# A recurrent attention layer and a soft-max feed-forward layer on one core: the same work in another written order

## The chip, the cores and the metric

The kernel runs on one core of one Trainium2 chip. Time is device microseconds (us) from the first to the last instruction of a run; the figure for a kernel is the median of its runs. A core has five engines with a queue each: TensorE (PE, matrix products into the banks of PSUM), VectorE (DVE), ScalarE (ACT), GpSimd (POOL) and SyncE (SP, which here only issues transfers). Each engine works through its queue in order and waits at an instruction until what it needs is there.

## The reference

Two layers, one after the other. The first is a linear recurrence over 768 steps for 4 batches and 8 heads of 48 columns; the second is a feed-forward layer over the 3072 tokens that come out.

```
for t in range(S):
    cur = einsum('bhd,bhe->bhde', u * k[t], v[t])
    y[t] = einsum('bhd,bhde->bhe', r[t], state + cur)
    state = w[t][..., None] * state + einsum('bhd,bhe->bhde', k[t], v[t])
x = y laid out as tokens x 384
h = x @ w_in                                   # 384 -> 1024
solu = h * softmax(h)
ln = (solu - mean(solu)) / sqrt(var(solu) + 1e-6) * g_ln
out = ln @ w_out                               # 1024 -> 384
```

Inputs and output are float32; the products are taken in bf16.

## The kernel before, in words

The recurrence is cut into chunks of 128 steps: 6 chunks for each of 4 batches make 24 units, numbered chunk by chunk, so that unit i needs the state that unit i-4 left. Every unit goes through some 35 stages, and every stage is a small function that issues its instructions on one engine. Nothing is looped over units in the code: the string ORDER at the top lists about 900 words, one for a stage of a unit, and the last loop of the kernel calls the stages in this order. `InOrder` ties every instruction of an engine to the one before it, so the words of one engine are its program, word for word. The order was found by a search outside the kernel, against a model of the engines' and the transfers' times.

A word is a stage name, a unit and, after a dot, a letter or a PSUM slot. The letters a, d, p, s name the engine or queue (ACT, DVE, POOL, SP). The slots s0 to s3 are single PSUM banks, b0 and b1 are pairs of banks. A slot is free for its next tile only when the last reader of the tile before it is done, so the slots too tie the engines together. The stages that matter:

- LW, LK, LR, LV: the loads of w, k, r and v of one unit (192 KB each; functions `load_w` to `load_v`, from line 230). LI and LO load the weights, LU and LG the small vectors.
- lw (ACT, logarithm), cum (PE, two products of 384 columns), ex (ACT, exponential inside the bank), kp (DVE, decay times k and r; `scaled`, line 313).
- p, q (POOL), dg (DVE), dv (POOL): the bonus term with u; vb (ACT or POOL): v cast to bf16.
- krk, krr (PE, four transposes each, line 335) and kr (ACT or DVE, the copy out of PSUM, line 350). For some units KD takes their place: a transposing transfer issued by SP (line 441).
- M (PE, eight products, line 354), m (DVE with the mask in it, or ACT followed by sel on POOL), Y (PE, `attend`, line 376), y (line 398). With the letter i in Y's word, dv enters as one more product of 384 columns and y is a plain copy on ACT; without it, y on DVE adds dv.
- S (PE), et (ACT), st (DVE): the state.
- X (PE) and xT (copy), or XD (a transposing transfer): y turned for the second layer.
- H (PE, `hidden`, line 458), e (ACT, exponential), he (DVE, h times e), hq (ACT, square). For the units that have a word HD (14 to 22) H is laid out by token, SP turns he by a transposing transfer (line 469), and the sums of e and of the squares come from ACT.
- Oa, Ob (PE, the two halves of the output product, line 495), sq (ACT), qm (DVE), lv (ACT), o (ACT or DVE) and out (the store). Unit 23, the last, is done in smaller pieces: Ha, Hb, ea, eb, hea, heb, hqa, hqb, Sa, Sb for the sums, and Mal, Mbl, Mar, Mbr for the left and right columns of its output.
- gw (ACT or POOL), mn (PE), ce (DVE), wi: the weights with the gain g_ln in them, less their column means, cast to bf16; once, in the first 40 us.
- hot: `warm_up` (line 292), dummy products of 512 columns on zeros, whose result nobody reads. They keep PE busy in the head, where its real work has gaps. hot3.s0 is three of them in bank s0.

Buffers go round: 7 for the loads, 10 for lw and vb, 6 for kp, kr and dv, 4 for the rest (line 71).

Of the kernel before, what the change touches and what calls it, by code (L numbers as in the profile page):

```python
# [31 lines left out]
e3 Oa0.s1 p6 y4.a LR9.s kr6.d cum7.b0 lw8 Oa1.s0 vb6.p he3 et4 ex7 dv5 Ob0 LW10.s hq2 q6 kp7 X4.s3 hq3 LK10.s
M5.b1 p7 xT4.d M6.b0 m5.d krk7.s3 Ob1 sq0 m6.a q7 LR10.s qm0 dg6 krr7 lw9 cum8.b1 LV8.p kr7.d lv0 H4.b0 LW11.s
ex8 st4 p8 dg7 sq1 o0.a LK11.s Y5.ns3 qm1 kp8 e4 Oa2.s2 out0.p LR11.s y5.d q8 krk8.s1 lv1 cum9.b1 he4 krr8 LV9.s
ex9 Ob2 p9 kr8.d lw10 S5.s3 p10 hq4 kp9 Oa3.s1 LW12.s sel6 sq2 o1.d et5 lw11 M7.b0 LK12.s M8.b1 qm2 st5 m7.a Ob3
dv6 m8.d lv2 q9 cum10.b0 LR12.s sq3 X5.s0 Y6.ns3 o2.d ex10 vb7.p cum11.b1 xT5.d S6.s2 vb8.a out1 sel7 qm3 kp10
ex11 Oa4.s0 y6.d LW13.s LV10.p et6 lv3 H5.b0 st6 lw12 dg8 LK13.s o3.a dv7 kp11 X6.s3 krk9.s1 e5 LV11.p LR13.s
krk10.s2 krr9 xT6.d cum12.b1 dg9 LW14.s kr9.a Ob4 q10 he5 ex12 Y7.is3 LK14.s LV12.p dg10 krk11.s1 sq4 y7.a krr10
kp12 krr11 p11 kr10.a M9.b0 LR14.s S7.s3 m9.d dv8 H6.b1 hq5 p12 qm4 kr11.d et7 LW15.s lv4 S8.s2 st7 e6 vb9.p
X7.s1 o4.d LK15.s M10.b0 dv9 Y8.ns3 et8 xT7.d lw13 krk12.s0 he6 m10.a Oa5.s1 out2.p LR15.s vb10.p krr12 lw14  # L40
y8.d cum13.b0 p13 H7.b1 st8 LW16.s ex13 kr12.d q11 hq6 kp13 LK16.s S9.s3 LV13.p Y9.ns2 e7 dg11 LV15.s M11.b0
y9.d LV14.p X8.s0 Ob5 et9 m11.a he7 vb11.p krk13.s2 LR16.s lw15 M12.b0 q12 st9 xT8.a cum14.b1 m12.d sq5 krr13
LW17.s ex14 X9.s0 vb12.p Oa6.s3 sel10 xT9.a qm5 kp14 LK17.s cum15.b0 lv5 Ob6 dv10 ex15 kr13.d S10.s0 lw16 p14
kp15 hq7 M13.b1 LR17.s Y10.ns2 q13 H8.b0 sq6 et10 vb13.a qm6 o5.d LW18.s sel11 lv6 y10.d m13.a krk14.s1 st10
LK18.s Oa7.s2 q14 dg12 e8 o6.d krr14 LR18.s dv11 Y11.ns0 kr14.d lw17 cum16.b1 dv12 X10.s3 he8 Ob7 ex16 LW19.s
p15 S11.s1 LV16.s sq7 y11.d xT10.a H9.b0 hq8 out3.p kp16 LV17.s p16 et11 st11 X11.s0 H10.b1 e9 LK19.s dg13 p17
xT11.d lw18 qm7 he9 LR19.s q15 Y12.ns3 vb14.a krk15.s1 e10 S12.s0 vb15.p out4 y12.d krr15 dv13 lv7 M14.b0 kr15.d
Oa8.s3 m14.a sel13 he10 out5 X12.s1 lw19 M15.b0 LW20.s q16 et12 Ob8 m15.a st12 LK20.s dg14 p18 cum17.b1 dg15
H11.b0 out6 ex17 xT12.d sel14 o7.d hq9 kp17 out7 krk16.s0 Y13.ns1 vb16.p LR20.s sq8 e11 krr16 dv14 qm8 H12.b1
LW21.s kr16.d q17 hq10 y13.d LK21.s he11 krk17.s2 dv15 Oa9.s0 e12 LR21.s vb17.p Y14.ns1 lv8 he12 krr17 LW22.s  # L50
o8.a M16.b0 Ob9 lw20 kr17.d m16.a out8 cum18.b1 y14.d X13.s3 Oa10.s2 ex18 dg16 xT13.d dv16 sq9 hq11 S13.s1 kp18
X14.s3 sel15 M17.b0 xT14.d et13 hq12 KD18 Ob10 qm9 m17.d p19 cum19.b1 S14.s3 st13 ex19 q18 H13.b0 lv9 kp19 sel16
sq10 o9.a Y15.ns1 et14 e13 out9 st14 H14.b1 p20 LV18.s y15.d lw21 qm10 LV19.s he13 Oa11.s0 LK22.s e14 dg17
X15.s3 cum20.b0 lv10 xT15.d Y16.ns1 he14 Ob11 o10.a ex20 out10 vb18.p S15.s2 y16.d dv17 KD19 sq11 S16.s3 kp20
et15 hq13 cum21.b1 q19 S17.s1 qm11 st15 LV20.s H15.b0 et16 lv11 q20 st16 LR22.s ex21 dg18 vb19.a krk20.s2 kp21
Oa12.s3 et17 e15 st17 KD21 M18.b1 o11.a krr20 he15 X16.s1 Ob12 m18.a LW23.s kr20.d S18.s0 xT16.a HD14 sel18 sq12
lw22 M19.b0 qm12 M20.b1 m19.d Y17.ns2 m20.a vb20.p LK23.s Oa13.s1 dv18 LR23.s lv12 dg19 cum22.b0 y17.d H16.b1
dv19 LV21.s ex22 o12.d sel20 et18 kp22 X17.s2 HD15 S19.s3 e16 st18 p21 Ob13 xT17.d et19 he16 krk22.s0 p22 sq13
lw23 M21.b0 krr22 m21.a Y18.ns2 st19 q21 HD16 cum23.b1 qm13 kr22.d Y19.ns3 ex23 sel21 H17.b0 y18.d LV22.s lv13
y19.d o13.a kp23 X18.s0 Oa14.s2 e17 xT18.d KD23 M22.b1 dg20 Ob14 hq14 he17 dv20 X19.s3 Y20.ns1 vb21.p hq15  # L60
Oa15.s0 dg21 HD17 q22 y20.d H18.b0 xT19.d sq14 hq16 dv21 m22.d XD20 Ob15 p23 e18 dg22 Y21.ns1 out11 qm14 H19.b1
# [564 lines left out]
```

## Time and profile before

| | |
|---|---|
| time, median of 3 runs | 146.9 us (146.39 to 147.08) |
| span of the profiled execution | 144.8 us |
| PE busy | 132.1 us, 91% |
| DVE busy | 126.3 us, 87% |
| ACT busy | 123.8 us, 85% |
| POOL busy | 102.2 us, 71% |
| moved by transfers | 30.65 MB, mean 212 GB/s |
| mean granted TensorE clock | 0.988 |

How to read it. "Busy" is the time in which an engine has at least one instruction in flight. The page cuts the span into 40 slices of 3.6 us and gives the busy share of each in tenths; the same in microseconds can be had for any stretch. A table of waits says for which instruction an engine stood idle and whose end released it. The chain is followed back from the last instruction, at each step to what released it or to the instruction before it on its engine: what stands on it set the end of the run. In the rows of the timeline the first number is the start in us from the span's start, the second the duration, and a bracket at the end gives the idle time of the engine before it. Nearly all instructions carry line 88, that of the helper `InOrder`, so the rows are told apart by their tiles: o_ps is the output product, h_ps the hidden product, kr_ps the transposes, cum_ps the decays, m_ps the scores, y_ps and s_ps the attention output and the state, warm_ps the dummy products.

### The profile page before, as it was taken

The page shows a single profiled execution, that of the slowest core. Times are in us where ns is not written, and L with a number is a line of the kernel's source. Part 1 is how long each engine was busy: PE and PEld are TensorE (multiplying, and loading weights), DVE is VectorE, ACT ScalarE, POOL GpSimd, SP SyncE. Part 2 cuts the span into 40 slices and gives each one's busy share as a digit, 9 for nine tenths or more (in the row PEclk, how much of TensorE's full clock was granted, in tenths as well). Part 3 has the DMA queues.
Part 4 walks back from the last instruction along what each step waited for, and adds up shares of the span by engine and source line. Part 5 has one row for each costly group of instructions (what it writes and reads, how often), then busy time and mean ns, then how long its engine had stood idle before and what let it go on. Part 6 is the DMA issues. An engine that isn't in the chain of part 4 may idle for free.

```text
span 144.8 us, 4709 instructions
## 1 busy us (share of the span) xinstructions
PE 132.1 (91%) x1824; PEld 95.7 (66%) x1832; DVE 126.3 (87%) x239; ACT 123.8 (85%) x269; POOL 102.2 (71%) x128
## 2 busy tenths in 40 slices
PE   6699848896999999999999999999999999999781
PEld 2135537675978778987789788777676656557460
DVE  7154999699999999999999999989999998998651
ACT  3457687798899999999998999988997999999881
POOL 5269989897892999999999997594459777300000
PEclk9999996999999999999999999999999999999999
DMA  4999999999999979999989979649699997976934
GB/s 93 269 260 263 304 400 363 235 206 217 260 187 231 240 161 239 237 210 217 238 166 233 256 193 201 153 100 203 144 219 161 217 132 174 229 174 121 250 142 163
DMA packets 105623, 30.65 MB, mean 212 GB/s; under 512 B 100553, under 2 KB 104402, under 8 KB 105602
## 3 DMA queue, kind: packets, MB, share of 16 engines
q1 hardware_dynamic: 100192, 26.12, 83.1%
q0 software_dynamic: 1088, 3.34, 7.3%
q10 hardware_dynamic: 4322, 0.89, 2.9%
q8 instruction: 14, 0.23, 0.7%
q14 instruction: 7, 0.06, 0.1%
HBM read 22.03 MB, written 4.72 MB: 185 GB/s over the span
## 4 chain that ended last, share of the span: by engine, by line
PE 80%; DVE 8%; DMA 6%; issue 2%; ACT 1%; SPq 0%; DVEq 0%
PE o_ps L88 24%; PE h_ps L88 21%; PE kr_ps L88 7%; PE cum_ps L88 6%; PE y_ps L88 6%; PE m_ps L88 6%; PE s_ps L88 6%; DMA hq<-he 3%; DMA w_in<-in_w_dram 3%; PE warm_ps L88 3%; PE x_ps L88 2%; DVE m L88 2%; DVE kp L88 2%; DVE w L88 1%; DVE he L88 1%
## 5 line engine op out<-in xcount | busy, mean ns | idle before, releaser
L88 DVE TENSOR_TENSOR he<-h_ps,e 128x1024 bf16<-128x1024 f32 (+1 forms) x25 | 29.4, 1177 | 1.8 <-ACT e L88 1.2
L88 PE MATMUL o_ps<-w,he 128*128 128x385 bf16 (+2 forms) x136 | 29.2, 306 | 0.4 <-DVE qm L88 0.4
L88 DVE TENSOR_TENSOR kp<-cum_ps,kr_in 128x768 bf16<-128x768 f32 x24 | 22.8, 952 | 5.2 <-ACT cum_ps L88 3.6
L88 ACT ACTIVATE e<-h_ps 128x1024 bf16<-128x1024 f32 (+1 forms) x25 | 24.7, 989 | 2.9 <-PE h_ps L88 2.7
L88 POOL TENSOR_TENSOR p<-kr_in 128x384 bf16<-128x384 f32 x24 | 23.9, 1003 | 4.3 <-DMA kr_in<-in_k_dram 2.9
L88 PEld LDWEIGHTS <-hq 128*128 128x128 bf16 x192 | 17.9, 97 | 12.6 <-DMA hq<-he 1.2
L88 POOL TENSOR_TENSOR dv<-vb,dg 128x384 bf16<-128x384 bf16 x24 | 19.9, 830 | 6.5 <-DVE dg L88 5.5
L88 PE MATMUL h_ps<-xT,win_sb 128*128 128x128 bf16 x360 | 23.4, 223 | 0.6 <-DVE kp L88 0.6
L88 ACT ACTIVATE cum_ps<-cum_ps 128x768 f32<-128x768 f32 x24 | 19.2, 799 | 4.3 <-PE cum_ps L88 3.6
L88 PEld LDWEIGHTS <-win_sb 128*128 128x128 bf16 x360 | 21.8, 100 | 1.5 <-issue 0.7
L88 POOL TENSOR_TENSOR q<-p,u_bc 128x384 bf16<-128x384 bf16 x24 | 21.8, 913 | 0.1
L88 PE MATMUL o_ps<-inv_col,e 128*128 128x1 bf16 x120 | 19.3, 165 | 0.0
L88 PE MATMUL o_ps<-one_col,hq 128*128 128x1 bf16 x120 | 19.1, 163 | 0.0
L88 PEld LDWEIGHTS <-kp 128*128 128x128 bf16 x240 | 15.5, 99 | 4.9 <-DVE xT L88 1.7
L88 DVE TENSOR_TENSOR m<-m_ps,uts 128x1024 bf16<-128x1024 f32 x13 | 15.8, 1219 | 2.4 <-PE m_ps L88 2.4
L88 PE MATMUL kr_ps<-ident,kp 128*128 128x128 bf16 x160 | 15.2, 226 | 1.6 <-DVE xT L88 1.6
L88 ACT ACTIVATE hq<-he 128x1024 bf16<-128x1024 bf16 (+1 forms) x16 | 15.9, 1003 | 0.0
L88 ACT ACTIVATE lw<-w_in 128x384 bf16<-128x384 f32 x24 | 12.6, 527 | 3.2 <-DMA w_in<-in_w_dram 3.2
L88 PE MATMUL o_ps<-w,hq 128*128 128x385 bf16 x72 | 13.9, 328 | 0.8 <-DMA hq<-he 0.8
L88 POOL TENSOR_SCALAR_AFFINE_SELECT m<-m 128x1024 bf16<-128x1024 bf16 x11 | 12.0, 1088 | 3.6 <-ACT m L88 3.6
L88 PEld LDWEIGHTS <-kr 64*128 64x128 bf16 (+1 forms) x272 | 10.7, 96 | 4.8 <-issue 1.1
L88 DVE TENSOR_REDUCE dg<-q 128x8 f32<-128x384 bf16 x24 | 13.0, 543 | 0.9 <-POOL q L88 0.9
(88 smaller groups left out, 309.8 us busy)
## 6 DMA issues: line engine op xcount, KB each, us to landing
kr_in<-in_r_dram SPq DMA_DIRECT2D x23, 192.0 KB, 4.5
kr_in<-in_k_dram SPq DMA_DIRECT2D x23, 192.0 KB, 4.3
w_in<-in_w_dram SPq DMA_DIRECT2D x22, 192.0 KB, 4.2
out_dram<-o SPq DMA_DIRECT2D x20, 192.0 KB, 2.2
v_in<-in_v_dram POOLq DMA_DIRECT2D x14, 192.0 KB, 4.3
v_in<-in_v_dram SPq DMA_DIRECT2D x10, 192.0 KB, 3.8
win_f<-in_moe_w_in_dram SPq DMA_DIRECT2D x3, 512.0 KB, 7.1
wout_f<-in_moe_w_out_dram SPq DMA_DIRECT2D x2, 768.0 KB, 9.7
```

Of the source, the lines that this page charges most:

```text
L88: made = make(*args, **kwargs)
```

## The change

ORDER is replaced by another one. The functions, the buffers, the number of slots and the rules of the queues stay. The search that wrote it put more weight on transfers that land later than planned, and counted the dummy products at half clock in the head. The diff swaps all 53 lines of the string; its first and last lines:

```diff
--- before.py
+++ after.py
@@ -19,53 +19,53 @@
 ORDER = """
-pc0 LU0.a LR0.s LW1.a LW0.s hot7.s3 LK0.s LK1.s LV0.p ur0 LW3.s LR2.s lw0 LW2.a cum0.b0 lw1 hot1.s3 LR1.a LW4.s
-cum1.b1 p0 ex0 us0.s0 hot2.s3 LV1.p LK2.a kp0 ex1 vb0.p krk0.s1 LK3.s uc0 hot3.s3 lw2 LR3.s LG0.a cum2.b0 p1 kp1
-krr0 hot3.s3 kr0.a LK4.s q0 LR4.s ex2 M0.b1 LV2.p krk1.s2 dg0 S0.s3 lw3 m0.d krr1 et0 hot5.s1 vb1.a LV3.p lw4
-kr1.d LI0.s p2 kp2 LI1.s gs0.s0 cum3.b1 q1 LI2.s S1.s1 st0 ex3 LO0.s M1.b0 Y0.ns2 q2 m1.d LW5.s krk2.s3 gc0 krr2
-LO1.s dv0 kr2.a LK5.s dg1 cum4.b0 p3 y0.d ex4 kp3 X0.s0 p4 et1 wi0.a dg2 M2.b1 krk3.s2 kp4 q3 Y1.ns3 krr3 kr3.a
-dv1 m2.d wi1.p vb3.a xT0.d LR5.s dg3 wi2.a krk4.s0 vb2.p M3.b0 st1 krr4 q4 y1.d Y2.ns1 S2.s2 m3.d H0.b1 dv2
-gw1.a LV4.p kr4.d et2 gw3.a LW6.s dg4 M4.b0 lw5 dv3 X1.s3 m4.d e0 hot3.s0 gw2.p gw0.a y2.d cum5.b0 LK6.s Y3.ns0
-xT1.d gw4.a gw6.p S3.s1 y3.d X2.s3 gw5.a he0 LR6.s gw7.a ex5 mn0.s0 LW7.s st2 et3 xT2.a kp5 vb4.p hq0 H1.b1 dv4
-ce4 LK7.s lw6 ce6 p5 ce1 cum6.b0 LR7.s X3.s2 ce7 krk5.s3 LV5.p ex6 ce3 krr5 LW8.s xT3.a kp6 q5 e1 S4.s2 LK8.s
...
-y21.d LV23.s vb22.a he18 lv14 XD21 dv22 Y22.ns3 e19 Oa16.s1 q23 y22.d out12 M23.b0 sq15 hq17 HD18 he19 Ob16
-Oa17.s3 vb23.p hq18 dg23 out13 H20.b1 o14.d dv23 HD19 qm15 m23.d lv15 X22.s2 sq16 Ob17 e20 out14 xT22.d H21.b0
-qm16 hq19 he20 Y23.ns2 sq17 e21 qm17 H22.b1 HD20 o15.d y23.d lv16 he21 lv17 Oa18.s0 e22 X23.s2 Ob18 HD21 xT23.d
-hq20 Oa19.s2 he22 Ha23.b0 sq18 hq21 Ob19 qm18 o16.d HD22 o17.d Hb23 lv18 Oa20.s1 sq19 out15 ea23 o18.d out16
-hq22 Oa21.s3 hea23 out17 Ob20 qm19 out18 eb23 Ob21 lv19 heb23 Oa22.s0 sq20 hqa23 qm20 o19.d sq21 lv20 Ob22 qm21
-out19 hqb23 o20.d Sa23.s2 sq22 lv21 qm22 out20 Mal23.s1 lv22 Sb23 o21.d sq23 o22.a Mar23.s3 out21 qm23 Mbl23
-lv23 out22 Mbr23 ol23.a or23.d outl23.a outr23
+pc0 LR0.s LU0.a LW1.a LW0.s hot7.s3 LK0.s LK1.s LV0.p ur0 LW3.s lw0 LR2.s LW2.a cum0.b0 lw1 us0.s0 LR1.a p0
+cum1.b1 ex0 hot3.s3 LW4.s LV1.p uc0 kp0 LK3.s LK2.a ex1 q0 krk0.s1 hot1.s3 lw2 LR3.s vb0.p LG0.a cum2.b0 hot2.s3
+lw3 p1 kp1 ex2 LK4.s krk1.s2 q1 krr0 LR4.s S0.s3 lw4 kr0.d cum3.b1 LV2.p krr1 vb1.a hot5.s0 kr1.a kp2 p2 ex3
+LI0.s dg0 krk2.s0 q2 et0 M0.b0 dg1 LI1.s hot4.s2 m0.d LI2.s dv0 LO0.s LV3.p kp3 LW5.s M1.b0 krr2 LO1.s p3 kr2.a
+st0 cum4.b1 LK5.s Y0.is1 m1.d gs0.s2 dv1 ex4 krk3.s0 y0.a vb2.p M2.b0 kp4 gc0 krr3 wi0.a p4 Y1.is3 kr3.d krk4.s1
+wi1.a q3 m2.d M3.b1 krr4 S1.s2 LV4.p X0.s0 LR5.s wi2.a dg2 kr4.d q4 y1.a m3.d S2.s1 xT0.a dv2 M4.b0 et1 Y2.ns3
+gw0.a X1.s0 dg3 gw3.p H0.b1 et2 m4.d gw1.p LW6.s lw5 y2.d e0 cum5.b0 st1 vb3.p xT1.d ex5 he0 dv3 S3.s3 Y3.ns2
+LK6.s gw2.a X2.s0 gw7.p gw6.a st2 H1.b1 LR6.s gw4.a dg4 y3.d gw5.a vb4.p xT2.d et3 hq0 mn0.s1 st3 LW7.s p5 kp5
+X3.s2 LK7.s LV5.p lw6 ce4 xT3.a ce0 cum6.b0 krk5.s0 LR7.s dv4 ce7 ex6 S4.s3 ce2 krr5 LV6.p e1 Y4.is2 LW8.s kp6
...
+hq17 Oa16.s1 LV23.s he18 XD21 X20.s0 H19.b1 sq15 lv14 xT20.d o14.d HD18 M23.b0 dg23 e19 Ob16 qm15 m23.d out13
+Y22.ns0 sq16 vb23.p lv15 Oa17.s3 out14 hq18 dv23 y22.d H20.b0 qm16 he19 lv16 Ob17 o15.d e20 HD19 X22.s0 H21.b1
+xT22.d sq17 hq19 he20 Y23.ns2 e21 o16.d Oa18.s0 HD20 qm17 y23.d H22.b0 hq20 he21 out15 X23.s1 Ob18 e22 HD21
+xT23.d Oa19.s2 sq18 lv17 he22 Ha23.b1 hq21 Ob19 qm18 o17.d HD22 Oa20.s1 lv18 sq19 Hb23 ea23 qm19 o18.d out16
+lv19 Ob20 out17 hq22 o19.d Oa21.s3 out18 hea23 out19 eb23 Ob21 sq20 hqa23 qm20 Oa22.s0 heb23 lv20 Sa23.s2 sq21
+hqb23 Ob22 qm21 o20.d lv21 Sb23 out20 sq22 Mar23.s1 qm22 o21.d sq23 lv22 Mbr23 qm23 out21 o22.d lv23 Mal23.s3
+Mbl23 or23.d out22 ol23.a outr23 outl23.a
 """
```

What differs word by word, apart from the places:

- Dummy products: hot7, 1, 2, 3, 3, 5, 3 (24) become hot7, 3, 1, 2, 5, 4 (22). The last group stood behind X1, near 27 us; now it stands between M0 and M1.
- Unit 20: krk20, krr20 and kr20 (PE, DVE) become KD20 (a transfer); XD20 (a transfer) becomes X20 and xT20 (PE, DVE).
- Y0, Y1 and Y6 take the letter i, and y0, y1 and y6 go from DVE to ACT; y4 and y7 had it before.
- kr0, kr3, kr9 and kr10 go from ACT to DVE; kr1, kr6 and kr15 from DVE to ACT. m15 and m20 go to DVE, m17 and m19 to ACT with sel17 and sel19 on POOL, in place of sel15 and sel20.
- vb3, vb8, vb13, vb14, vb19 and vb22 go from ACT to POOL; vb12 and vb17 from POOL to ACT. LV9 goes from SP's queue to POOL's.
- wi1 goes from POOL to ACT; gw1, gw3 and gw7 from ACT to POOL; gw2 and gw6 from POOL to ACT.
- xT0 goes to ACT, xT2 and xT9 to DVE, xT6 to ACT; o4, o5 and o7 go to ACT, o9, o13 and o22 to DVE.
- PE's program near the end was Ob18 Oa19 Ha23 Ob19 Hb23 Oa20 Oa21 Ob20 Ob21 Oa22 Ob22 Sa23 Mal23 Sb23 Mar23 Mbl23 Mbr23; it is Ob18 Oa19 Ha23 Ob19 Oa20 Hb23 Ob20 Oa21 Ob21 Oa22 Sa23 Ob22 Sb23 Mar23 Mbr23 Mal23 Mbl23.
- The stores of units 0, 8, 9 and 10 (out0, out8, out9, out10) are issued much later in the order.

More of the change, by code (lines that the diff above doesn't have):

```diff
@@ L27 @@
-dv1 m2.d wi1.p vb3.a xT0.d LR5.s dg3 wi2.a krk4.s0 vb2.p M3.b0 st1 krr4 q4 y1.d Y2.ns1 S2.s2 m3.d H0.b1 dv2
-gw1.a LV4.p kr4.d et2 gw3.a LW6.s dg4 M4.b0 lw5 dv3 X1.s3 m4.d e0 hot3.s0 gw2.p gw0.a y2.d cum5.b0 LK6.s Y3.ns0
-xT1.d gw4.a gw6.p S3.s1 y3.d X2.s3 gw5.a he0 LR6.s gw7.a ex5 mn0.s0 LW7.s st2 et3 xT2.a kp5 vb4.p hq0 H1.b1 dv4
-ce4 LK7.s lw6 ce6 p5 ce1 cum6.b0 LR7.s X3.s2 ce7 krk5.s3 LV5.p ex6 ce3 krr5 LW8.s xT3.a kp6 q5 e1 S4.s2 LK8.s
-ce5 H2.b0 LV6.p kr5.a he1 LR8.s lw7 krk6.s3 ce0 e2 H3.b1 LW9.s ce2 dg5 vb5.p hq1 LV7.p st3 krr6 Y4.is0 LK9.s he2
@@ L32 @@
[L32 to L61, printed above, removed]
@@ new lines @@
+y4.a q5 ce3 LK8.s H2.b0 kr5.a he1 p6 LR8.s lw7 X4.s2 et4 ce1 krk6.s0 e2 LV7.p H3.b1 ce5 ce6 hq1 LW9.s q6 he2
+krr6 Oa0.s1 e3 p7 dg5 LK9.s cum7.b0 kr6.a q7 he3 Ob0 LR9.s ex7 vb5.p Oa1.s0 xT4.d st4 hq2 LW10.s p8 M5.b1 kp7
+Ob1 hq3 dv5 m5.d krk7.s2 LK10.s lw8 M6.b0 q8 krr7 m6.a dg6 cum8.b1 LR10.s vb6.p S5.s3 kr7.d sq0 ex8 H4.b0 dg7
+LW11.s p9 dg8 et5 sq1 lw9 qm0 st5 lv0 LK11.s sel6 Y5.ns2 kp8 e4 Oa2.s3 LR11.s dv6 qm1 cum9.b1 o0.a he4 Ob2 lw10
+LV8.p LW12.s lv1 krk8.s1 y5.d ex9 M7.b0 vb7.p LK12.s o1.d krr8 p10 Oa3.s2 sq2 m7.a qm2 kr8.d LR12.s X5.s0 kp9
@@ new lines @@
+LV9.p lv2 Y6.is1 hq4 LW13.s M8.b0 xT5.d LV10.p cum10.b1 m8.d Ob3 lw11 ex10 q9 krk9.s0 LK13.s o2.d cum11.b0 y6.a
+krr9 kp10 sel7 sq3 ex11 S6.s3 LR13.s S7.s1 qm3 lw12 kp11 vb8.p H5.b1 et6 lv3 out1 dv7 st6 o3.a LV11.p kr9.d et7
+cum12.b0 krk10.s3 st7 ex12 LW14.s Oa4.s2 out0.p e5 kp12 X6.s0 LV12.p krr10 Y7.is1 LK14.s xT6.a he5 Ob4 vb9.p
+y7.a lw13 p11 LR14.s M9.b0 sq4 kr10.d hq5 X7.s0 krk11.s1 dv8 H6.b1 qm4 dg9 lv4 m9.d q10 LW15.s o4.a krk12.s3
+out2.p e6 krr11 xT7.d LK15.s M10.b0 kr11.d p12 S8.s2 m10.a he6 S9.s0 Y8.ns1 dv9 LR15.s et8 lw14 krr12 cum13.b0
@@ new lines @@
+dg10 et9 p13 H7.b1 y8.d ex13 LW16.s kr12.d vb10.p LK16.s kp13 q11 lw15 Y9.ns1 Oa5.s3 e7 st8 sel10 st9 cum14.b0
+hq6 LR16.s X8.s2 y9.d Ob5 vb11.p he7 ex14 LV13.p LW17.s S10.s0 xT8.a Oa6.s1 kp14 p14 hq7 LK17.s S11.s2 dg11 dv10
+et10 LR17.s sq5 M11.b1 lw16 st10 M12.b0 m11.a Ob6 q12 qm5 m12.d LW18.s et11 q13 krk13.s0 cum15.b1 st11 krr13
+ex15 H8.b0 sel11 kr13.d LK18.s lv5 kp15 dv11 o5.a LR18.s krk14.s2 X9.s0 dg12 e8 M13.b1 p15 krr14 xT9.d LW19.s
+Y10.ns3 kr14.d sq6 m13.a Oa7.s0 q14 qm6 y10.d LV15.s vb12.a Y11.ns2 LV14.p he8 cum16.b1 lv6 LV16.s Ob7 lw17
@@ new lines @@
+vb13.p o6.d ex16 out3.p X10.s3 LV17.s H9.b0 y11.d xT10.a q15 dg13 sq7 hq8 LK19.s kp16 krk15.s1 X11.s2 e9 krr15
+vb14.p xT11.d H10.b1 dv12 kr15.a he9 out4 dv13 Oa8.s3 e10 out5 qm7 sel13 dg14 LR19.s M14.b0 lv7 he10 Y12.ns2 p16
+m14.a Ob8 LW20.s y12.d o7.a sel14 M15.b0 S12.s1 lw18 LK20.s m15.d lw19 cum17.b1 dv14 krk16.s2 ex17 X12.s0 out6
+krr16 xT12.d H11.b0 p17 kr16.d sq8 hq9 out7 kp17 q16 LR20.s et12 Y13.ns0 e11 LW21.s st12 Y14.ns2 vb15.p H12.b1
+dg15 p18 hq10 y13.d LK21.s he11 q17 lw20 X13.s1 Oa9.s0 LR21.s e12 dv15 qm8 y14.d M16.b0 lv8 LV18.s he12 krk17.s2
@@ new lines @@
+vb16.p Ob9 o8.a LW22.s m16.a krr17 xT13.d cum18.b1 kr17.d S13.s1 ex18 X14.s3 dg16 cum19.b0 et13 xT14.d Oa10.s2
+hq11 dv16 kp18 S14.s3 p19 sq9 ex19 st13 KD18 M17.b1 Ob10 et14 hq12 q18 kp19 LV19.s Y15.ns1 sel16 qm9 lw21 st14
+H13.b0 LK22.s m17.a dg17 LR22.s y15.d lv9 dg18 sel17 H14.b1 sq10 e13 KD19 qm10 o9.d vb18.p lv10 S15.s3 he13 q19
+LW23.s e14 X15.s1 Oa11.s0 p20 xT15.d et15 vb17.a cum20.b0 he14 S16.s1 o10.a p21 Ob11 ex20 st15 vb19.p cum21.b1
+kp20 dv17 sq11 lw22 S17.s2 ex21 Y16.ns3 dg19 q20 KD20 H15.b0 et16 qm11 y16.d et17 hq13 p22 st16 out8 kp21
@@ new lines @@
+Oa12.s3 lv11 dv18 LV20.s e15 st17 out9 M18.b1 Ob12 KD21 m18.a he15 X16.s1 Y17.ns2 sq12 xT16.a sel18 LK23.s
+M19.b1 dg20 o11.a M20.b0 LR23.s y17.d Oa13.s1 m19.a q21 HD14 qm12 m20.d S18.s0 lv12 sel19 cum22.b1 dg21 X17.s2
+out10 H16.b0 ex22 o12.d HD15 dv19 et18 kp22 q22 Ob13 e16 LV21.s xT17.d dg22 LV22.s M21.b1 st18 krk22.s3 m21.a
+S19.s2 he16 krr22 Y18.ns0 et19 sq13 sel21 lw23 H17.b1 hq14 y18.d HD16 st19 vb20.p kr22.d cum23.b0 dv20 X18.s0
+Y19.ns2 ex23 xT18.d Oa14.s3 qm13 y19.d e17 vb21.p Y20.ns0 kp23 X19.s2 p23 Ob14 hq15 he17 KD23 H18.b0 dv21 lv13
@@ new lines @@
+xT19.d vb22.p y20.d HD17 sq14 hq16 M22.b1 dv22 qm14 o13.d Oa15.s2 m22.d q23 e18 Y21.ns0 out11 Ob15 out12 y21.d
+hq17 Oa16.s1 LV23.s he18 XD21 X20.s0 H19.b1 sq15 lv14 xT20.d o14.d HD18 M23.b0 dg23 e19 Ob16 qm15 m23.d out13
+Y22.ns0 sq16 vb23.p lv15 Oa17.s3 out14 hq18 dv23 y22.d H20.b0 qm16 he19 lv16 Ob17 o15.d e20 HD19 X22.s0 H21.b1
+xT22.d sq17 hq19 he20 Y23.ns2 e21 o16.d Oa18.s0 HD20 qm17 y23.d H22.b0 hq20 he21 out15 X23.s1 Ob18 e22 HD21
+xT23.d Oa19.s2 sq18 lv17 he22 Ha23.b1 hq21 Ob19 qm18 o17.d HD22 Oa20.s1 lv18 sq19 Hb23 ea23 qm19 o18.d out16
```

## The prediction

> **What bounds the kernel now.** I read the busy shares first, then the table by stage, then the chain that ended last, and last the timeline at both ends.
>
> ```profile
> PE 132.1 (91%) x1824; PEld 95.7 (66%) x1832; DVE 126.3 (87%) x239; ACT 123.8 (85%) x269; POOL 102.2 (71%) x128
> ...
> PE   6699848896999999999999999999999999999781
> ...
> DVE  7154999699999999999999999989999998998651
> ...
> POOL 5269989897892999999999997594459777300000
> PEclk9999996999999999999999999999999999999999
> ```
>
> No engine stands out over the whole span, so the shares alone decide nothing: three engines are full from about a quarter of the span to a tenth before its end. The slices show three stages, a ragged head, a full body and a thinning tail.
>
> ```profile
> core 0: us, PE busy (x) PEld busy (x) DVE busy (x) ACT busy (x) POOL busy (x), PEclk, DMA share, GB/s
> 10.00:20.00 10.00, 8.30 (x90) 4.76 (x90) 8.07 (x12) 5.98 (x12) 9.98 (x12) 1.00 1.13 308
> 20.00:30.00 10.00, 7.72 (x112) 6.10 (x112) 8.68 (x15) 8.19 (x14) 8.70 (x11) 0.83 1.03 299
> 30.00:40.00 10.00, 8.75 (x137) 7.52 (x136) 10.00 (x17) 8.84 (x14) 8.58 (x11) 1.00 1.07 233
> 40.00:130.00 90.00, 89.65 (x1369) 67.56 (x1374) 87.18 (x148) 85.39 (x189) 70.33 (x85) 1.00 0.94 197
> 130.00:145.00 15.00, 10.35 (x107) 7.13 (x105) 8.21 (x18) 10.68 (x37) 0.00 (x0) 1.00 0.66 168
> ```
>
> In the 90 us of body PE idles 0.35 us, DVE 2.8, ACT 4.6. Only less work helps there, or a start or an end that is tighter. PE's records overlap, so its 89.65 hides some slack: 24 hidden products take 1.34 us on the chain. Adding such chain prices for all PE words between the first and the last but two outputs gives 91 us for the 95 us they took. So PE has about 4 us of slack, DVE about 3.
>
> ```profile
> 24.63 2.06 PE h_ps L88 x24
> ...
> 44.72 1.34 PE h_ps L88 x24
> ...
> 130.77 4.79 DMA hq<-he
> 135.56 0.05 issue
> 135.60 3.50 PE o_ps L88 x20
> ...
> 140.47 1.17 PE o_ps L88 x12
> ```
>
> The same 24 products cost 2.06 us at 24.6 and 1.34 later: the clock dip of the seventh slice. In the tail the chain leaves PE for 4.79 us: the transposed transfer of unit 21 (HD21), issued once he21 is done. Behind it stand five half outputs (20 matmuls), then the last unit's pieces.
>
> ```profile
> 1.64 2.77 PE L88 MATMUL warm_ps<-warm 128*128 128x512 bf16 x6
> ...
> 14.25 1.03 PE L88 MATMUL warm_ps<-warm 128*128 128x512 bf16 x4
> ...
> 46.66 0.61 POOL L88 DMA_DIRECT2D out_dram<-o  x1 [2.61 <-ACT o L88]
> ...
> 140.45 1.17 PE L88 MATMUL o_ps<-w,he 128*128 128x192 bf16 x12 [0.45 <-DVE qm L88]
> ```
>
> The first row gives 0.43 us per dummy product while the clock is low, the second about 0.22 once it is up. POOL loses 2.61 us in front of the store of unit 0. In the last row PE waits 0.45 us for bank s3, which o21 still holds (the row names qm; the DVE operation that really frees s3 is the o at 139.78, done at 140.40).
>
> **What the Trainium skill says.** "TensorE: Matmul & The Clock Gate", section "What's actually happening": the array runs at half clock until a free-running window of about 3.4 us was busy, and falls back after an idle one. The trace agrees: the clock is 0.65 in 22 to 24 us, 0.50 in 24 to 26, 0.99 in 26 to 28, after PE had stood idle for 1.57 us before 22.36. "DMA: Bandwidth & Descriptors", section "DMA Transpose (X-bar)": such transfers go out from the Sync or Scalar queue only, and two transposing streams may not be in flight together. Here all 15 stand in SP's order, so a late one holds the next. "SBUF — State Buffer", section "SBUF: two separate sides": GpSimd and a VectorE operation with two SBUF inputs lock each other out. The trace shows no sign of it, since the 17 POOL casts lie between 494 and 517 ns, and I price moved casts so.
>
> **The change, part by part.** No instruction kind is new; prices are the mean durations of before.
>
> *Totals.* DVE: three y additions go (Y0, Y1, Y6 take dv through PE and are copied by ACT), 3 x 0.55 = -1.65; xT20 comes, +0.35; kr, m and o keep their counts. Sum -1.30. ACT: vb 7 to 3 (-2.02), kr 6 to 5 (-1.01), gw 6 to 5 (-0.61), y 2 to 5 (+1.46), wi 2 to 3 (+1.04): -1.14. POOL: four casts (+2.02), one gain (+1.25), one load issue LV9 (+0.93), one w_in cast less (-1.04): +3.2. PE: two dummies fewer (22 for 24), eight transposes of unit 20 fewer (0.22 per four: -0.45), three of X20 (+0.17), three ident products of 384 columns (0.16 each, +0.5): level but for the dummies. Transposed transfers stay 15: KD20 comes, XD20 goes.
>
> *Head.* I step through it with those durations, landing times kept. LW0 lands at 5.22 in both. After it: cum0, u, cum1, three dummies, krk0 to 9.1, cum2 about 10.1. LR1 lands at 9.98, so kp1 ends at 10.94, krr0 about 12.1. kr0 is now on DVE (0.68 in place of 1.01 on ACT) and ends at 12.9, where ACT ended it at 12.91. But M0 now takes bank b0, which kp2 must leave (13.9), and stands behind hot5 and krk2: about 14.8, where it was 12.96. That is 1.8 us later on m0; DVE fills it with kp2, dg0 and dg1. Then DVE runs m0 to 16.4, kp3 17.4, st0, m1 19.1, kp4 20.1, kr3, m2 21.9, dg2, kr4, m3 24.3, dg3, m4 26.1, y2, st1, xT1, he0 28.7; then st2, dg4, y3, xT2, st3, kp5 32.1. Before: he0 ended at 30.84, kp5 at 32.17. H0 waits for xT0 and the third w_in cast in both, about 24.4. So the head is level: **0 us**. Its ends: -1 if H0 meets the full clock (2.06 against 1.34, and the 1.19 us that DVE waited for M behind it), +1.5 if the clock rises one window of 3.4 us later, when hot5 and hot4 cost 0.43 in place of 0.22 each (nine, 1.9 us), partly under DVE's work.
>
> *Body.* From kp5 to he22, DVE has 107.5 us of work by this price list where it had 108.9: -1.4. PE keeps its work to within 0.1. DVE can give at most the 1.3 that it is rid of, and nothing if PE binds; both are full. I take a quarter, **-0.3**. POOL's extra: gw3, gw1 and gw7 lie before 30 us; LV9, vb8, vb13 and vb14 less vb12 add 1.9 in the window 46 to 89 where POOL never paused; against it out0 is issued far later, behind o0, and the 2.61 us wait goes. Level there; after 89 us POOL has over 15 us to spare. Moved casts are thus hidden. ACT's smaller load is hidden by its 4.6 us of idle.
>
> *Tail.* PE's order was Ob19 Hb23 Oa20 Oa21(waits) Ob20 Ob21 Oa22 Ob22; now Ob19 Oa20 Hb23 Ob20 Oa21(waits) Ob21 Oa22 Sa23 Ob22. Ob20 (four matmuls, 0.66 on the chain) moves in front of the wait: -0.66. HD20 was not waited for when Oa20 came at 133.95; now Oa20 comes 0.66 earlier, and if it waits, Hb23, ea23 and hea23 queue behind it; bounds 0 and 0.66, I take 0. The last pieces are now Mar Mbr Mal Mbl, so that bank s3 is asked for two pieces later, with o21 itself earlier: the 0.45 us wait goes. Sum **-1.1**, between 0 (HD21 lands later, since out15 is issued ahead of it) and -1.5 (Sa23 also moves into the gap).
>
> Sum: 146.9 - 0 - 0.3 - 1.1 = **145.5 us**.
>
> **The rivals.** *The tail is eaten* (20%): HD21 ends the tail whatever stands before it, and 4.79 us becomes 5.8 behind out15; -0.3 remains, 146.6. For it: SP holds transposes and stores in one order. Against it: he21 is issued no later, and one store adds some 0.6 us of issue. *A new wait in head or body, slower* (20%): the head pays the later clock (+1.5), or POOL's 3.2 us come out as late dv and vb, so that Y and S wait; with -0.5 of tail left, 147.9. For it: POOL at 9.98 of 10 between 10 and 20 us, and dv2 and dv3 now behind more casts and gains. Against it: 2.61 us of old wait removed. *The clock is better* (10%): -1 in the head, 144.5.
>
> **How the numbers follow.** Forecast 50%, rivals 20, 20 and 10. Low: the last rival with another 0.6 us of DVE's saving, 143.9. High: the slower rival, 147.9. Faster by over 0.5% (under 146.2): 0.50 + 0.10 = 0.60; within: 0.21; slower: 0.19.
>
> **What would show it.** Right: kp5 ends near 32 us; DVE idles under 2.8 us in the body; the wait for HD21 comes after Ob20 with four half outputs behind it, and no wait for s3. Wrong: a clock of 0.5 after 26 us, PE waiting on hq20 before Hb23, or POOL named by waits on y, S or Y between 46 and 89 us.

## The result, and the profile after

The changed kernel takes 147.7 us (146.4 to 150.2, 17 runs) where the kernel before, run in turn with it, takes 146.9 us (145.9 to 147.4, 17 runs). The ratio on record is 1.0077 with a 95% interval of 1.005 to 1.0104, the ratio of the two medians 1.0053: slower by 0.5 to 0.8%, where 145.5 us had been forecast. Measured twice more, the ratio came to 1.0018 (0.9992 to 1.0043) and 1.0032 (1.0005 to 1.0059), that of the medians to 1.0039 and 1.0038. The ratios on record leave out runs more than 1.5% above the fastest of their kernel, among them four of the changed kernel's 22 in the first repetition, so 1.0018 understates it.

The busy slices of the changed kernel, as they were shown of before:

```profile
PE 130.5 (89%) x1821; PEld 94.8 (65%) x1828; DVE 125.6 (86%) x237; ACT 122.2 (84%) x267; POOL 105.0 (72%) x133
...
PE   6597887478998999999999999999999999999980
...
DVE  7146999898998999989899899999999999997480
...
POOL 5279995999939999999897599799967665300000
PEclk9999999999999999999999999999999999999999
```

Every engine but POOL has less work, as the sums of the prediction said, and in this trace the clock shows no dip. Yet the span is 145.9 us where it was 144.8. The slices of DVE hold eights where before they held nines. The table by stage says where:

```profile
10.00:20.00 10.00, 8.30 (x100) 5.13 (x99) 8.32 (x11) 6.48 (x11) 9.42 (x11) 1.00 1.10 303
20.00:30.00 10.00, 6.46 (x126) 5.60 (x124) 9.30 (x15) 7.80 (x16) 8.28 (x10) 1.00 0.98 286
30.00:40.00 10.00, 8.58 (x128) 7.09 (x126) 9.34 (x16) 8.80 (x15) 9.86 (x13) 1.00 1.06 225
40.00:130.00 90.00, 88.37 (x1350) 66.83 (x1353) 85.49 (x144) 82.87 (x184) 72.02 (x89) 1.00 0.98 201
130.00:145.00 15.00, 11.53 (x111) 7.53 (x109) 9.04 (x21) 11.04 (x38) 0.00 (x0) 1.00 0.64 172
```

(Columns as before: PE, PE's weight loads, DVE, ACT, POOL, then clock, DMA share and GB/s.) In the 90 us of body PE now idles 1.63 us where it idled 0.35, DVE 4.5 in place of 2.8, ACT 7.1 in place of 4.6. The body has gained holes.

One word tells the stages apart: he, DVE's product of each unit. In the table below, he3 is where the head ends, he22 where the tail begins; the last column runs from the start of he22 to the landing of the last store.

| trace | he3 starts | he3 to he4 | he4 to he5 | he5 to he6 | he6 to he8 | he8 to he22 | he3 to he22 | after he22 |
|---|---|---|---|---|---|---|---|---|
| before | 40.5 | 6.9 | 9.5 | 5.5 | 13.4 | 55.5 | 90.8 | 12.5 |
| changed, first trace | 39.5 | 8.2 | 10.4 | 4.9 | 14.0 | 55.7 | 93.3 | 11.8 |
| changed, second | 39.5 | 7.5 | 10.4 | 4.3 | 13.2 | 55.7 | 91.2 | 11.8 |
| changed, third | 38.8 | 8.4 | 10.4 | 4.3 | 14.0 | 55.7 | 92.8 | 11.8 |

Beside this one trace of before, he3 comes 1.0 to 1.7 us earlier, the tail is 0.7 us shorter, and the body 0.4 to 2.5 us longer. (Part of the lead at he3 belongs to the clock: the trace of before has a stretch at half speed at 22.6 us, see the end.) What makes one and the same order vary by 2 us is read in the waits of the first trace of the changed kernel, 35 to 75 us (us in total, times, the longest):

```profile
POOL p L88 <- DMA kr_in<-in_r_dram: 2.5, 1, 2.5
...
ACT lw L88 <- DMA w_in<-in_w_dram: 1.5, 1, 1.5
...
ACT o L88 <- DMA out_dram<-o: 0.6, 1, 0.6
DVE dg L88 <- POOL q L88: 0.6, 1, 0.6
ACT lv L88 <- DVE qm L88: 0.6, 1, 0.6
```

Three of them are transfers. The kernel before has in the same stretch no wait for r or w at all; its largest is the known one at the store of unit 0:

```profile
POOL out_dram L88 <- ACT o L88: 2.6, 1, 2.6
```

How a load reaches the body is seen in the timeline of the changed kernel, POOL, DVE and ACT each (start, duration, and the idle time before):

```profile
42.89 1.00 POOL L88 TENSOR_TENSOR p<-kr_in 128x384 bf16<-128x384 f32 x1 [2.52 <-DMA kr_in<-in_r_dram]
...
44.63 0.91 POOL L88 TENSOR_TENSOR q<-p,u_bc 128x384 bf16<-128x384 bf16 x1
```
```profile
45.58 0.55 DVE L88 TENSOR_REDUCE dg<-q 128x8 f32<-128x384 bf16 x1 [0.63 <-POOL q L88]
46.05 0.15 DVE L88 TENSOR_TENSOR qm<-o_ps,sq 128x1 f32<-128x1 f32 x1
```
```profile
46.23 0.29 ACT L88 ACTIVATE lv<-sq,qm 128x1 f32<-128x1 f32 x1 [0.60 <-DVE qm L88]
...
46.67 1.00 ACT L88 ACTIVATE e<-h_ps 128x1024 bf16<-128x1024 f32 x1
```

This is one chain: r of unit 8 was issued at 35.90 and landed at 42.40; POOL stood 2.52 us at p8; so q8 came late; so DVE stood 0.63 us at dg8, ahead of qm0; so ACT stood 0.60 us at lv0, ahead of e4; so he4 was late. In the order before, dg8 comes behind qm0 to qm3, so lv0 doesn't wait behind it, and p8 started without a wait, 4.5 us after its load had landed (38.54):

```profile
43.03 1.02 POOL L88 TENSOR_TENSOR p<-kr_in 128x384 bf16<-128x384 f32 x1
```

The second one is ACT at lw15, which the changed order puts ahead of e7:

```profile
66.83 0.52 ACT L88 ACTIVATE lw<-w_in 128x384 bf16<-128x384 f32 x1 [1.50 <-DMA w_in<-in_w_dram]
67.26 1.00 ACT L88 ACTIVATE e<-h_ps 128x1024 bf16<-128x1024 f32 x1
```

In the tail, PE of the changed kernel shows what was forecast and one thing that was not:

```profile
131.61 1.49 PE L88 MATMUL o_ps<-w,hq 128*128 128x385 bf16 x8
132.94 0.83 PE L88 MATMUL h_ps<-xT,win_sb 128*128 128x128 bf16 x12
133.61 1.49 PE L88 MATMUL o_ps<-w,hq 128*128 128x385 bf16 x8
134.93 0.83 PE L88 MATMUL h_ps<-xT,win_sb 128*128 128x128 bf16 x12
135.60 0.83 PE L88 MATMUL o_ps<-w,hq 128*128 128x385 bf16 x4
136.68 1.50 PE L88 MATMUL o_ps<-w,hq 128*128 128x385 bf16 x8 [0.25 <-DMA hq<-he]
```

The wait for the transposed transfer of unit 21 is down to 0.25 us and stands behind Ob20 (the x4). But the x8 at 133.61 are Ob19 and Oa20, and the x12 behind them are Hb23: the last unit's hidden product comes one half output later, and ACT stands for it, where in the kernel before it did not wait (before first, then changed):

```profile
134.15 0.60 ACT L88 ACTIVATE e<-h_ps 128x512 bf16<-128x512 f32 x1
```
```profile
135.80 0.60 ACT L88 ACTIVATE e<-h_ps 128x512 bf16<-128x512 f32 x1 [0.95 <-PE h_ps L88]
```

That is 2.87 us after he22 before, and 3.01 after the change.

### The profile page after: what moved, and what is told of

It reads as the page before. It is cut to its first block, busy times and chain, and to the rows that moved or that the text cites. A ratio compares the mean times of both kernels' runs of the same rounds, so it can differ in the third digit from the quotient of the medians.

```text
span 145.9 us, 4697 instructions
## 1 busy us (share of the span) xinstructions
PE 130.5 (89%) x1821; PEld 94.8 (65%) x1828; DVE 125.6 (86%) x237; ACT 122.2 (84%) x267; POOL 105.0 (72%) x133
## 4 chain that ended last, share of the span: by engine, by line
PE 45%; DMA 17%; POOL 12%; SPq 10%; issue 6%; ACT 6%; DVE 1%; POOLq 0%; DVEq 0%; ACTq 0%
PE o_ps L88 15%; PE h_ps L88 14%; SPq L88 10%; DMA wout_f<-in_moe_w_out_dram 7%; DMA kr_in<-in_r_dram 4%; PE y_ps L88 4%; POOL v_in L88 3%; DMA out_dram<-o 3%; PE s_ps L88 3%; PE m_ps L88 3%; DMA w_in<-in_w_dram 3%; PE cum_ps L88 2%; PE kr_ps L88 2%; POOL p L88 2%; ACT e L88 2%
## 5 line engine op out<-in xcount | busy, mean ns | idle before, releaser
L88 PE MATMUL o_ps<-w,he 128*128 128x385 bf16 (+2 forms) x136 | 29.7, 306 | 0.6 <-DVE st L88 0.5
L88 PEld LDWEIGHTS <-hq 128*128 128x128 bf16 x192 | 17.6, 97 | 12.6 <-ACT hq L88 1.0
L88 PE MATMUL h_ps<-xT,win_sb 128*128 128x128 bf16 x360 | 22.7, 219 | 0.5 <-DVE kp L88 0.5
L88 PEld LDWEIGHTS <-win_sb 128*128 128x128 bf16 x360 | 20.9, 98 | 1.1 <-issue 0.6
L88 PEld LDWEIGHTS <-kp 128*128 128x128 bf16 x232 | 15.0, 98 | 6.6 <-DVE kp L88 2.2
L88 POOL CAST vb<-v_in 128x384 bf16<-128x384 f32 x21 | 10.6, 504 | 7.6 <-DMA v_in<-in_v_dram 4.0
L88 PE MATMUL kr_ps<-ident,kp 128*128 128x128 bf16 x152 | 14.7, 222 | 0.9 <-DVE kp L88 0.9
L88 POOL DMA_DIRECT2D v_in<-in_v_dram x15 | 14.0, 932 | 0.0
```

The lines of the kernel that those rows point to most:

```text
L88: made = make(*args, **kwargs)
```

## The experiments

The theory after this reading: words of the changed body stand ahead of needed work and wait for loads that arrive late, differently in each execution; besides, Oa20 ahead of Hb23 takes back part of the tail's gain. Rivals: the head and its clock; the order of the work in the body, whatever the loads do.

**The changed kernel again, and hybrids of the two orders.** In the first hybrid the first 213 words are the changed ones and the rest is the order before; in the second the words up to o16 are the old ones and the rest is the changed order. The third is the changed order with three words moved away from the waits above:

```
-  p9 dg8 et5 ... he4 Ob2
+  p9 et5 ... he4 dg8 Ob2
-  LV8.p LW12.s ... Oa4.s2 out0.p e5
+  LV8.p out0.p LW12.s ... Oa4.s2 e5
-  q11 lw15 Y9.ns1 Oa5.s3 e7 st8
+  q11 Y9.ns1 Oa5.s3 e7 lw15 st8
```

> The changed kernel once more, unaltered, as a second reading of its trace. In the first reading it led the kernel before by 1.0 us at he3 (39.5 against 40.5) and lagged by 1.3 us at he5 (58.1 against 56.9), and three waits on transfers lie between: POOL 2.5 us for r of unit 8, ACT 0.64 us for the store of unit 0, ACT 1.5 us for w of unit 15. Theory (the new order stands closer to its transfers): the same waits, or others on transfers between 38 and 70 us, and a time near 147.7. Rival (a chance stall of that one execution): no wait over 0.5 us on a transfer in that stretch, and a time under 147.0.

> The new order up to its 213th word (the load of k of unit 9, about 37 us), then the words that are left in the order of before. Theory (the head is better, the loss arises behind it): the lead of 1.0 us at he3 is kept, 145.9 us. Rival (the new head pays by issuing its loads 1 to 2 us later, the body starves whatever its order): 146.9 us or more, with waits on transfers between 40 and 70 us.

> The order of before up to o16, then the words that are left in the new order (Oa20 ahead of Hb23, Ob20 ahead of Oa21, right columns of the last unit first). As predicted: -1.1, 145.8 us. Theory after the result (the end is set by ScalarE's chain behind Hb23, which now starts four products later): -0.3 to -0.4, 146.5 us. Rival (the new tail costs): 147.2 us or more.

> The changed kernel with three words moved: dg8 from ahead of qm0 to behind he4 (DVE no longer waits for POOL's late q8 ahead of qm0, lv0 and e4), out0 from behind LV11 to behind LV8 on POOL (its store is out before o4 needs the buffer), lw15 from ahead of e7 to behind it (ACT no longer waits for w of unit 15 ahead of e7). Theory (these waits on late data are the loss): 1.5 to 2.3 us faster than the changed kernel, 145.4 to 146.2 us. Rival (ACT has 1.3 us more of its work placed ahead of e5, the order of the work itself is the loss): no change, 147.5 to 147.7 us.

Measured: the changed kernel 1.0018 (0.9992 to 1.0043), new head 1.0038 (1.0016 to 1.006), new tail 1.001 (0.9982 to 1.0038), three words moved 1.0124 (1.0087 to 1.0161). The second trace of the changed kernel has a wait of 2.2 us at p8 and loses nothing by it, so neither of its two expectations came true as it stood. The new head on the old order missed 145.9 us; it took the time of its rival, yet its trace has the old body, 90.8 us to the tenth, with no wait for r or w in it. The three moved words were a plain miss: a version that should have been faster is a further 1% slower. In its trace neither late load delays he any more (he3 to he4 7.5 us, he6 to he8 13.3), but he4 to he5 took 10.9 in place of 10.4, and the last store landed 12.6 us after he22 in place of 11.8, though it was issued at the same time. That trace is of the fastest of its ten runs, so the rest of the loss isn't seen. The new tail on the old body gave nothing: there ea23 starts 3.55 us after he22, where it was 2.87 before.

**Hb23 put back; the old head; light loads.** The first is one word moved:

```
-  o17.d HD22 Oa20.s1 lv18 sq19 Hb23 ea23
+  o17.d HD22 Hb23 Oa20.s1 lv18 sq19 ea23
```

The second has the first 213 words of before and then the changed order (seven bank numbers had to be changed to fit). The other two, before and after, have the loads of units 7 to 23 cut to a quarter, with the same issues and the same arithmetic, on data that is partly old:

```
-  queue[x].dma_start(out=w_t[i % NIO][:, :, :D], in_=rows_of(w, i))
+  def hs(i): return slice(0, H if i < NIO else 2)                                    # NIO is 7
+  queue[x].dma_start(out=w_t[i % NIO][:, hs(i), :D], in_=rows_of(w, i)[:, hs(i), :])  # k, r and v likewise
```

> The changed order with one move: Hb23 goes back in front of Oa20. Nothing else differs. If the last unit's ScalarE chain (ea23, the squares, hqa23, hqb23) sets the end, as the trace of the changed kernel suggests, Hb23 ends 0.66 us earlier and so does the kernel: about 0.6 us below the changed kernel as it was, ratio to the kernel before about 0.998. If the transfer of he21 sets the end instead, nothing is gained or 0.2 us is lost.

> The first 213 words of the order before (its head, its dummies), then the changed order. If the head is where the loss lies (the new head alone on the old rest gave 1.0038), this is level with the kernel before: 0.999 to 1.001, and spreads no more than it. If late transfers in the body of the new order make the loss, it stays at 1.004 to 1.008.

> The kernel before with the loads of k, r, v and w of units 7 to 23 cut to two of eight heads (the buffers keep older data, so the computation of those units is not the reference's). Issues, order and arithmetic work stay. If late landings hold the body, it becomes faster, by 0.5 to 1 us; if engine work holds it, it stays within 0.3 us.

> The changed kernel with the same light loads. Theory of late transfers in the body: the loss of the change goes, and it comes out level with or below the light kernel before, with its runs no more scattered. Rival, the order of work itself or the head: it stays 0.5 to 1 us above the light kernel before.

Measured: Hb23 put back 0.9968 (0.9943 to 0.9993); old head 1.0063 (1.0037 to 1.0088); before, light 1.0001 (0.9978 to 1.0024); changed, light 0.9982 (0.9953 to 1.001). The light loads do nothing for the kernel before, and with them the changed kernel comes out level: that points to the late transfers, and the next experiment sets it beside the changed kernel itself. The move of Hb23 turns the loss into a gain, by a little more than expected. The old head should have been level if the head alone were at fault, and it isn't. But this doesn't clear the head. With the old head the loads came earlier, p8 and lw15 waited for none, and the body took 91.8 us through waits of its own, which the changed order doesn't have: 0.5 us of PE's weight load for a copy kr, 0.4 us of ACT for m_ps. The hybrid thus has a loss at its seam, of another kind.

**Which loads, and is the gain at Hb23 a matter of the tail?** Light loads for units 7 to 13 alone, then for 14 to 23 alone; the old order up to o16 with the changed tail and Hb23 put back; and the changed kernel beside them.

> The changed kernel with the loads of k, r, v and w of units 7 to 13 alone cut to two of eight heads (those units compute on older data); units 14 to 23 load in full. If the late transfers that cost the change lie between 30 and 65 us (r of unit 8, v of units 8 and 9, w of unit 15's place in the queue), this is as good as with all loads light: 0.997 to 0.9995 of the kernel before. If they lie later, it stays at 1.002 to 1.006.

> The changed kernel with the loads of units 14 to 23 alone light; units 7 to 13 load in full. The mirror image: stays at 1.002 to 1.006 of the kernel before if the loss lies between 30 and 65 us, comes down to 0.997 to 0.9995 if it lies in the later loads.

> The order before up to o16, then the changed order with Hb23 put back in front of Oa20. The old body doesn't depend on late transfers. If the changed tail is worth about 1 us once Hb23 isn't held back (new tail as it was: 1.001), this runs at 0.993 to 0.996 of the kernel before. If the gain of moving Hb23 came from something in the changed body, it stays at 0.998 to 1.001.

> The changed kernel unaltered, beside the others. 1.002 to 1.008 of the kernel before by every theory; it fixes the level from which the gains of the light loads and of Hb23 are counted.

Measured: 0.9967 (0.9945 to 0.999) with units 7 to 13 light, 1.0002 (0.9979 to 1.0026) with the later ones light, 0.9997 (0.9964 to 1.003) for the old order with the mended tail, 1.0032 (1.0005 to 1.0059) for the changed kernel, all timed beside each other. Most of the loss comes with the loads of units 7 to 13: 0.65%, 0.95 us. The scatter goes with it: the changed kernel ran between 145.8 and 147.9 us, with units 7 to 13 light between 145.4 and 146.9 (22 runs each). The waits of that trace, 35 to 75 us, name no load at all:

```profile
POOL m L88 <- ACT et L88: 1.8, 1, 1.8
ACT cum_ps L88 <- PE cum_ps L88: 1.1, 2, 0.6
DVE kp L88 <- ACT cum_ps L88: 0.3, 1, 0.3
```

and ACT reaches lv0 and e4 without the 0.60 us:

```profile
45.10 0.31 ACT L88 ACTIVATE lv<-sq,qm 128x1 f32<-128x1 f32 x1
...
45.55 1.01 ACT L88 ACTIVATE e<-h_ps 128x1024 bf16<-128x1024 f32 x1
```

The stage table of this kernel for the body shows what the order is worth when no load holds it:

```profile
40.00:130.00 90.00, 89.58 (x1359) 67.65 (x1363) 86.80 (x148) 85.12 (x188) 70.62 (x88) 1.00 0.80 167
```

PE is as full as before (89.65), and DVE idles 3.2 us where before it idled 2.8. The old order with the mended tail missed its expectation of 0.993 to 0.996. Its trace, of the fastest of its 14 runs, shows ea23 at 2.87 us after he22 again, but an o on DVE now waits for an earlier store to leave its buffer:

```profile
DVE o L88 <- DMA out_dram<-o: 1.3, 1, 1.3
```

so its tail is 12.6 us to the last landing, against 11.1 to 11.2 in the changed order. In these traces the mended tail pays only behind the order that leads up to it.

**The three words one at a time**, on the version with Hb23 put back.

> The changed order with Hb23 in front of Oa20 (0.9968 of the kernel before) and one more move: dg8, the sum on VectorE that needs r of unit 8, goes behind he4. If VectorE standing at dg8 for a late r is a main part of the loss (0.7 to 0.9 us between he3 and he4 in the two disturbed traces), this gains 0.4 to 0.8 us: 0.991 to 0.994. If the delay only moves to the next word, or if this move is what made the version with all three moves slow, it is 0.997 to 1.003.

> The same base, and lw15, ScalarE's logarithm that needs w of unit 15, goes behind e7. If ScalarE standing at lw15 is a main part (0.8 us between he6 and he8 in the two disturbed traces, none in the others), 0.2 to 0.5 us on average: 0.993 to 0.9955. Otherwise level with the base at 0.996 to 0.998.

> The same base, and out0, the store of unit 0 on GpSimd's queue, goes up behind LV8, so that o4 finds its buffer free. The trace shows 0.6 to 0.8 us between he5 and he6 for o4's wait in three of the traces. If that counts, 0.2 to 0.5 us: 0.993 to 0.9955. If GpSimd standing at the store again, as it did for 2.6 us in the kernel before, holds up dv and vb behind it, this is the move that made the version with all three slow: above 1.0.

Measured: dg8 behind he4 1.0038 (1.0007 to 1.0069); lw15 behind e7 0.9979 (0.9947 to 1.001); out0 behind LV8 0.9993 (0.9962 to 1.0025); the base, timed in an earlier group of runs, stands at 0.9968. The changed kernel alone moved between 1.0018 and 1.0077 from group to group, so small differences to the base decide nothing; the other two moves are level with it. That of dg8, 0.7% or 1 us above it, points to the move that made the three together slow. In both traces with it he3 to he4 is at its floor of 7.5, he4 to he5 is 10.9 in place of 10.4, and the last store lands 0.8 us later than in the same order without it (12.6 for 11.8, 11.9 for 11.1). Why it lands later stays open. Besides, the trace of dg8 alone has 1.4 us of ACT at lw15, and 14.15 us from he6 to he8. The wait at dg8 is where the late load shows; moving that word away doesn't mend it.

**Has the head a part in it, and do the two causes add?** The old head with the changed rest and Hb23 put back; the new head on the old order with units 7 to 13 light; the changed order with Hb23 put back and units 7 to 13 light.

> The head of the kernel before, the changed body and tail, and Hb23 back in front of Oa20. With the old head alone the changed order ran at 1.0063, although its loads were issued up to 4 us earlier. If the gain of moving Hb23 is the same whatever stands before it, 0.999 to 1.001. If the earlier loads of the old head matter, 0.992 to 0.996.

> The changed head on the old order (1.0038 with full loads), now with the loads of units 7 to 13 cut to two of eight heads (those units compute on older data). If the loss of that hybrid came from loads that the new head holds up, level with the kernel before or better: 0.997 to 1.000. If it came from the head's own work or the clock, it stays at 1.002 to 1.006.

> The changed order with Hb23 in front of Oa20, and the loads of units 7 to 13 light in the same way. If the two causes are separate and add, the body takes 91.2 us from he3 to he22 and the tail 9.5 us, and the kernel runs at 0.991 to 0.994. If moving Hb23 gained only what the late transfers had lost, it stays at 0.996 to 0.998.

Measured: 1.0011 (0.9977 to 1.0045), 1.0019 (0.9997 to 1.0041) and 0.9929 (0.9908 to 0.9949). The last is as expected: the causes are separate and add up, body 91.2 us, tail 9.5 us counted to the last issue on SP, 11.1 to the last landing. The old head keeps a loss of its own that Hb23 mends by 0.5%, as elsewhere; the new head with light loads lies between its two expectations.

The table of the traces that carry this, in the columns of the table above:

| trace | he3 starts | he3 to he4 | he6 to he8 | he3 to he22 | after he22 | ratio |
|---|---|---|---|---|---|---|
| before, light | 39.5 | 6.9 | 13.4 | 90.8 | 12.7 | 1.0001 |
| new head, old rest | 39.9 | 6.9 | 13.4 | 90.8 | 12.8 | 1.0038 |
| old order, mended tail | 38.7 | 6.9 | 13.4 | 90.8 | 12.6 | 0.9997 |
| changed, all light | 39.2 | 7.5 | 13.2 | 91.2 | 11.8 | 0.9982 |
| changed, 7 to 13 light | 39.1 | 7.5 | 13.2 | 91.2 | 11.8 | 0.9967 |
| Hb23 put back | 39.3 | 7.9 | 13.0 | 92.2 | 11.2 | 0.9968 |
| Hb23 put back, 7 to 13 light | 39.8 | 7.5 | 13.2 | 91.2 | 11.1 | 0.9929 |
| old head, changed rest | 39.3 | 7.8 | 13.2 | 91.8 | 12.1 | 1.0063 |

The old body takes 90.8 us in every trace, with full loads and light; the changed one takes 91.2 when the loads are light, and 91.2 to 93.3 when they are not. How a late load becomes a late he can be read off one for one. These are traces of the changed head and body with full loads, with the same words from he3 to e4:

| trace | p8 starts after he3 | he3 to he4 |
|---|---|---|
| changed, second | 2.70 | 7.52 |
| Hb23 put back, lw15 behind e7 | 3.02 | 7.84 |
| Hb23 put back | 3.12 | 7.95 |
| changed, first | 3.41 | 8.22 |
| changed, third | 3.57 | 8.40 |

Light, p8 starts 0.8 us after he3 or earlier, and he3 to he4 is 7.5. So POOL's wait at p8 costs nothing until p8 starts about 2.7 us after he3, and from there on he4 is late by what p8 is late. That is why the second trace waited 2.2 us at p8 for nothing. lw15 does the same to he8: in the first and the third trace it starts 3.79 and 3.75 us after he6, and he6 to he8 is 14.05 and 14.00; in the second it starts 2.74 us after, and he6 to he8 is 13.2.

## Why the prediction was wrong

**Head: right in the traces, not settled in the timed runs.** kp5 was to end at 32.1 us, level with before; it ended at 31.6, 31.5 and 30.8 in the three traces of the changed kernel. he3 starts between 38.7 and 40.5 with the old head and between 38.8 and 40.5 with the new. No dip of the clock came after 26 us in the three traces of the changed kernel; the same head had one from 28.3 us in another trace, with he3 at 40.5. Level in the traces is not level in the timed runs, though: the new head on the old order ran at 1.0038 (1.0016 to 1.006), with light loads at 1.0019. And the rival of a better clock came true in its clock, not in its time. Of the 291 runs of the kernel before in the experiments, 29 list a mean granted clock of 0.995 or more, and average 145.3 us; the 104 with 0.985 to 0.995 average 146.4. Of the changed kernel's 61 runs, 29 had 0.995 or more, but they average 147.2 us, and the 19 with 0.985 to 0.995 average 146.9. Its head meets the full clock more often, and its runs gain nothing by it. The third trace shows one way in which a gain is lost: he3 comes 0.7 us earlier than in the other two, r of unit 8 lands at 41.9 us all the same, and he3 to he4 is the longest of the three.

**Body: the step that failed.** "I take a quarter, -0.3" had both its size and its sense wrong. First, DVE's 1.3 us less of work bought nothing: undisturbed, the changed body takes 91.2 us where the old one takes 90.8, PE at 89.58 of 90 us and DVE idling 3.2. The prediction's 4 us of slack for PE, from prices on the chain, brought nothing; its other clause, nothing if PE binds, fits the stage table, but no run tests what binds the undisturbed body. That is +0.4. Second, and larger, the working never asked when the loads come. It checked engines and banks word by word and kept landing times fixed, and it didn't compare, for each early word of the new order, the landing of its data with its new start. p8 stood at 43.0 in the kernel before; the changed order asks for it at 40.4, while r of unit 8 is issued 1 us later (35.9 for 34.9) and lands 3.9 us later (42.4 for 38.5). The head has a share in that: in the traces with the old head and full loads this load landed 3.7 to 4.8 us after its issue, in those with the new head 4.9 to 6.5; why it takes longer isn't shown. dg8 moved from behind qm0 to ahead of it, and lw15 from behind e7 to ahead of it. With DMA engines busy 0.99 of the time between 40 and 60 us before, and 0.92 to 0.99 after, there was little slack for that. The cost in the three traces of the changed kernel is 2.1, 0 and 1.6 us over the undisturbed body, 1.2 us on average; light loads brought 0.95 us back in the timed runs.

**POOL's extra work hidden: right in the sum, wrong in what it hid.** POOL's 3.2 us did not come out as late dv or vb. The 2.61 us wait at out0 went, as said, and a wait of 2.2 to 2.8 us at p8 took its place; POOL passed a load's lateness on to DVE. The even times of POOL's casts, in which the prediction saw no sign of a lockout, are no test of one: in the trace of before each of DVE's operations on two tensors reads one of them from PSUM (kp reads cum_ps, m m_ps, he h_ps). The slower rival of the prediction, 147.9 us, thus had the place (a new wait in the body, by way of POOL) and, by luck, the time, but not the cause.

**Tail: the mechanism right, one term mis-sized.** From the start of he22 to the landing of the last store: before 12.5 us, changed 11.8, Hb23 put back 11.2. To the end of the span it is 13.5, 13.1 and 12.5, since the program's closing steps behind the last landing took 1.0 us before and 1.3 in the other two. Ob20 ahead of the wait and the wait for s3 were put at -0.66 and -0.45; with Hb23 put back the tail is 1.3 us shorter to the last landing and 1.0 to the end of the span, which is what these two had promised. "If it waits, Hb23, ea23 and hea23 queue behind it; bounds 0 and 0.66, I take 0" is the term that failed: Oa20 didn't wait, and still pushed Hb23 back by its own four matmuls. It took 0.6 us back. Moved ahead of a chain that sets the end, a product costs its duration without waiting for anything.

The sum as measured: body +0.4 and on average +1.2 for late loads, tail -0.4 to the end of the span: +1.2 us with the head set level, against 0.3 to 1.1 us in the three comparisons. Three traces make a rough average.

**What stays open.** The old head with the changed rest ran at 1.0063. Its body, 91.8 us with and without Hb23 put back, gives 0.9 us over before; its trace is of one of the fastest of its 22 runs (146.1, the median is 147.0), so what the others lost isn't seen. With Hb23 put back it ran at 1.0011, where the changed head has 0.9968. Open too is why the last store lands later when dg8 is moved. A trace shows one execution, and in this order executions differ by more than the things sought.

**A version that beats both** came out of it: the changed order with Hb23 put back in front of Oa20, 145.7 us (145.1 to 147.8, 22 runs) beside 146.3 for the kernel before, ratio 0.9968 (0.9943 to 0.9993). It was timed once, and the interval ends just below 1.
